# Pair-wise tap tables, wider tap matmuls and one-run Toeplitz loads in a kernel of attention and a state-space convolution

## The chip, the core and the metric

The kernel runs on one core of one Trainium2 chip. The metric is device time in microseconds for one launch, taken as the median of several runs. A profiled execution stands beside the runs; its span is what the views of the trace cover.

## What is computed

Sequence length 2,048, width 448. Two branches share the input layout and are mixed by a gate for each row (cut from the reference):

```python
g = sigmoid((x * gate_w).sum(-1, keepdims=True))
# branch A: attention, 16 query heads of 28 on one shared key and value head
scores = einsum("bhqd,bkd->bhqk", q, k) * 28 ** -0.5
a = (softmax(scores) @ v).reshape(B, S, 448) @ wo
# branch B: 448 channels, 256 complex modes each; taps K, then a causal convolution
P = exp((dt * (A_re + 1j * A_im))[:, :, None] * l)          # l = 0..2047
K = einsum("dn,dnl,dn->dl", Cc, P, dt * Bc).real
b = causal_conv(u, K) + u * Dskip                           # by FFT in the reference
out = g * a + (1 - g) * b
```

## The kernel before

All work is written as operations with dependences (`Prog.op`, `Prog.dma`), and `Prog.schedule` puts them into one fixed order per engine. It walks through the program with a planned duration for each operation and a priority `pr`; among what could start, the earliest goes first, and at equal times the lower `pr`. It also plans TensorE's code: instructions come in blocks of 256, and a new block is taken to need `FETCH` nanoseconds when the DMA is planned busy and `IDLE` when it is not (line 82, used in lines 201 to 221). Operations with `pr` of 1 or more may be held back for this. The engines then run their lists in order, with semaphore waits.

**Attention.** The scores of 16 row blocks (four heads of 512 rows each time) are cut into 1,024 tiles of 128 x 512. `qk` (lines 1095 to 1136) makes two or three tiles in up to five PSUM banks, on TensorE as 3 matmuls on 29 rows (line 1103) or as four column groups of 32 (line 1112); ScalarE takes the exponential of the two or three in one instruction (line 1134), and `pv` multiplies with the values (line 1144). VectorE evicts (line 1004) and scales by the denominators (line 1014), which take a detour through DRAM issued by GpSimd. `qproj` makes the queries (line 759), `outp` the output projection (line 986, folded in by line 995), three times four of them during the stream, and the fourth set in `tail` (line 1055).

**Taps.** The channels go in 14 blocks `c` of 32, with modes on the 128 partitions in two halves, so 64 columns for each power. `masters` (lines 780 to 818) squares the modes for a group of blocks. `tables(c)` builds, on VectorE, 32 powers by doubling: five levels `lv`, in each of which the existing `w` rows are multiplied by the real and imaginary master (lines 850 and 852) and combined (lines 854 and 856). `rho` (line 863) holds squared magnitudes, line 867 makes from it the second half of the moving operand, `Fm`, and line 872 turns the sign of the imaginary rows. In `tab` a row holds the 128 columns of one power, 256 bytes, so what one channel needs steps by 256 bytes.

`kgen(c)` (lines 875 to 912) turns the tables into taps: for each channel, over two halves of the modes and the real and imaginary part, a matmul with 32 stationary columns (one every row) and 64 moving ones. Four channels stand side by side in column groups of 32. That is 128 matmuls for 32 channels, all into one PSUM bank; VectorE adds the skip term (line 899) and evicts (line 902) into `kstg`, and nine transfers on GpSimd's queue write the taps to DRAM, in `KP_scratch`, which has a row of `KW` = 1,088 for each channel (and a shifted copy, `KH` further on).

**Convolution.** `tload` (lines 924 to 935) reads Toeplitz matrices from `KP_scratch`: four channels at a time, 128 partitions, each one element further into the row, as two transfers (even and odd partitions) of 64 partitions with four runs of 2,048 bytes. There are seven buffers (`tbufs`, lines 914 to 922): four in `T`, and three in `U` that come free as its channels are used up. 112 such loads are issued on SP's queue, in order, each when its buffer is free and its taps are in DRAM. `conv` (28 times, lines 937 to 978) runs 128 matmuls over four loads (line 949), scales (line 958), transposes back (line 969) and adds to `O` (line 977). It takes two of the two PSUM banks that groups share (`POOL`, line 85): one for the sums, one for the transposed result.

In the order of before the tap generation of the last block stands at exp tiles 940 to 955 of 1,024, and convolutions 22 and 23 of 0 to 27 at 925 to 940 and 960 to 968; convolutions 26 and 27 come after the last tile.

Of the kernel before, what the change touches and what calls it, by code (L numbers as in the profile page):

```python
# [24 lines left out]
BLK = 33 * EW  # L25
LO = 2 * BLK
# [8 lines left out]
TW = 4 * 1024  # L35
# [39 lines left out]
class Prog:  # L75
# [6 lines left out]
    BLOCK, FIRST, FETCH, IDLE, NEED = 256, 172, 5300.0, 3300.0, 0.015  # L82
# [48 lines left out]
    def dma(self, pairs, desc, slot, rd=(), wr=(), pr=0, eng="sp", slow=False, extra=0):  # L131
# [6 lines left out]
        o = self.op(eng, fn, nd * ns / 16.0 * (1.15 if size < 1500 else 1.8 if nd < 512 else 1.0), rd, wr, pr)  # L138
# [237 lines left out]
class Kernel:  # L376
# [25 lines left out]
    def alloc(self):  # L402
# [26 lines left out]
        self.T = sb("T", NTR * TW + 768, BF)  # L429
# [10 lines left out]
        self.kstg = sb("kstg", 2 * 256, BF)  # L440
# [44 lines left out]
    def loads(self):  # L485
# [62 lines left out]
        pg.dma([(self.skt.v(32 * g + 31, 1, 0, [[8, 14], [1, 8]]), dram(ins["B_Dskip"], 8 * g, [[16 * D, 1], [32, 14], [1, 8]]))  # L548
                for g in range(4)], (112, 8), "sk", rd=["skt"], wr=["skt"], pr=1, slow=True)
# [230 lines left out]
    def masters(self, b):  # L780
# [13 lines left out]
        for k in range(11):  # L794
# [20 lines left out]
            off = k * 256 if k < 5 else (k - 6) * 256 + 64  # L815
# [4 lines left out]
    def tables(self, c):  # L820
# [18 lines left out]
        done = [lk(1), lk(2)]
        for lv in range(5):  # L840
# [388 lines left out]
```

## Time and profile before

| | |
|---|---|
| median of 3 runs | 544.31 us (542.96 to 545.7) |
| profiled execution | 546.33 us; its span 544.5 us |
| granted TensorE clock, mean | 0.953 |
| ScalarE, exponentials (line 1134) | 410 instructions, 468.1 us |
| VectorE, busy | 455.3 us in 826 instructions |
| TensorE, tap generation (line 889) | 1,792 matmuls recorded |
| Toeplitz loads | 224 transfers of 512 KB, about 9.4 us from issue to landing |

The span is cut into 40 slices in the views that show digits; each digit is the busy share in tenths. A group's line gives the line in the code, engine, operation, what it writes and reads, shape, count, busy time, mean length in nanoseconds, and the idle time just before it with what ended it. "issue" is idle time for which the profile shows no one being waited for. Matmul lengths overlap each other; their pace is read from how long a row of them takes. "T<-KP_scratch" and "U<-KP_scratch" are the Toeplitz loads.

### The profile page before, as it was taken

The page shows a single profiled execution, that of the slowest core. Times are in us where ns is not written, and L with a number is a line of the kernel's source. Part 1 is how long each engine was busy: PE and PEld are TensorE (multiplying, and loading weights), DVE is VectorE, ACT ScalarE, POOL GpSimd, SP SyncE. Part 2 cuts the span into 40 slices and gives each one's busy share as a digit, 9 for nine tenths or more (in the row PEclk, how much of TensorE's full clock was granted, in tenths as well). Part 3 has the DMA queues.
Part 4 walks back from the last instruction along what each step waited for, and adds up shares of the span by engine and source line. Part 5 has one row for each costly group of instructions (what it writes and reads, how often), then busy time and mean ns, then how long its engine had stood idle before and what let it go on. Part 6 is the DMA issues. An engine that isn't in the chain of part 4 may idle for free.

```text
span 544.5 us, 20905 instructions
## 1 busy us (share of the span) xinstructions
PE 451.6 (83%) x9463; PEld 226.4 (42%) x9479; DVE 455.3 (84%) x826; ACT 485.9 (89%) x431; POOL 168.1 (31%) x313
## 2 busy tenths in 40 slices
PE   4787679688798989789788898889898898996875
PEld 3522114154353535345344445345454444352443
DVE  2889999999999989889989998989899999912024
ACT  3699899999999989899999999999999998997840
POOL 5017022515142413315215241515225060532100
PEclk9958888999999999899999999999899999998888
DMA  8995691696977697896994998798994999679996
GB/s 254 238 232 151 47 159 30 172 355 206 360 238 247 189 368 244 257 365 216 361 373 136 362 308 305 208 390 273 326 371 144 345 337 353 182 258 321 361 385 194
DMA packets 122401, 144.55 MB, mean 265 GB/s; under 512 B 54196, under 2 KB 60956, under 8 KB 122312
## 3 DMA queue, kind: packets, MB, share of 16 engines
q1 hardware_dynamic: 112312, 133.06, 75.9%
q0 software_dynamic: 9344, 9.59, 7.3%
q8 instruction: 74, 1.21, 0.9%
q10 hardware_dynamic: 656, 0.57, 0.4%
q14 instruction: 15, 0.12, 0.1%
HBM read 128.76 MB, written 5.28 MB: 246 GB/s over the span
## 4 chain that ended last, share of the span: by engine, by line
ACT 30%; PE 27%; DVE 19%; DMA 15%; issue 3%; SPq 0%
ACT expT L1134 30%; DMA T<-KP_scratch 9%; PE psS L1112 6%; DMA U<-KP_scratch 6%; PE psX L889 5%; PE psS L1103 4%; PE psB L1144 4%; PE psS L949 2%; PE psX L949 2%; DVE msq L796 2%; DVE tab L850 2%; DVE mbf L816 2%; DVE seedz L800 1%; PE psS L889 1%; DVE tmp L852 1%
## 5 line engine op out<-in xcount | busy, mean ns | idle before, releaser
L1134 ACT ACTIVATE expT<-psS 128x1536 bf16<-128x1536 f32 (+1 forms) x410 | 468.1, 1317 | 23.1 <-PE psS L1112 11.7
L1112 PE MATMUL psS<-qM,kT 128*32 128x512 bf16 x1660 | 134.3, 400 | 14.0 <-ACT expT L1134 10.6
L1103 PE MATMUL psS<-qT,kT 29*128 29x512 bf16 x609 | 82.9, 400 | 33.4 <-ACT expT L1134 29.6
L1144 PE MATMUL psB<-expT,vaug 128*32 128x512 bf16 x1024 | 104.7, 398 | 0.7 <-issue 0.4
L135 POOL DMA_DIRECT2D KP_scratch<-kstg x126 | 67.8, 546 | 70.7 <-DVE kstg L902 69.2
L850 DVE TENSOR_TENSOR tab<-tab,mbf 128x256 bf16<-128x256 bf16 (+4 forms) x70 | 68.6, 979 | 0.7
L1103 PEld LDWEIGHTS psS<-qT,kT 29*128 29x128 bf16 x609 | 19.9, 91 | 83.3 <-ACT expT L1134 72.9
L135 POOL DMA_DIRECT2D rdenB<-R_scratch x60 | 30.6, 517 | 75.8 <-DMA R_scratch<-denT 56.3
L889 PE MATMUL psX<-tab 128*32 128x64 bf16 x1280 | 49.5, 286 | 0.3 <-issue 0.2
L1112 PEld LDWEIGHTS psS<-qM,kT 128*32 128x32 bf16 x1660 | 30.4, 98 | 45.6 <-ACT expT L1134 34.7
L1144 PEld LDWEIGHTS psB<-expT,vaug 128*32 128x32 bf16 x1024 | 27.4, 96 | 49.9 <-issue 38.2
L135 POOL DMA_DIRECT2D qM<-qT x64 | 32.1, 509 | 43.4 <-DVE gt L638 20.4
L889 PEld LDWEIGHTS psX<-tab 128*32 128x32 bf16 x1280 | 39.4, 135 | 11.3 <-issue 3.9
L949 PE MATMUL psX<-T,U 128*32 128x128 bf16 (+7 forms) x1568 | 34.4, 221 | 9.0 <-DMA T<-KP_scratch 5.9
L135 POOL DMA_DIRECT2D denT<-acc x15 | 11.3, 756 | 97.5 <-DVE acc L1004 97.5
L949 PE MATMUL psS<-T,U 128*32 128x128 bf16 (+7 forms) x1216 | 30.2, 222 | 9.5 <-DMA T<-KP_scratch 6.7
L852 DVE TENSOR_TENSOR tmp<-tab,mbf 128x256 bf16<-128x256 bf16 (+3 forms) x56 | 36.3, 648 | 0.0
L949 PEld LDWEIGHTS psX<-T,U 128*32 128x32 bf16 (+7 forms) x1568 | 26.5, 94 | 20.3 <-DMA T<-KP_scratch 8.1
L867 DVE TENSOR_TENSOR tab<-tab,tmp 128x4096 bf16<-128x4096 bf16 x14 | 32.1, 2290 | 0.4
L852 DVE TENSOR_TENSOR tab<-tab,mbf 128x4096 bf16<-128x4096 bf16 x14 | 31.9, 2278 | 0.0
L949 PEld LDWEIGHTS psS<-T,U 128*32 128x32 bf16 (+7 forms) x1216 | 21.7, 95 | 21.0 <-DMA T<-KP_scratch 6.9
L863 DVE TENSOR_TENSOR tmp<-tmp,mq 128x64 bf16<-128x64 bf16 (+4 forms) x70 | 25.3, 361 | 1.2
(153 smaller groups left out, 553.4 us busy)
## 6 DMA issues: line engine op xcount, KB each, us to landing
T<-KP_scratch SPq DMA_DIRECT2D x174, 512.0 KB, 9.3
U<-KP_scratch SPq DMA_DIRECT2D x50, 512.0 KB, 9.5
rdenB<-R_scratch POOLq DMA_DIRECT2D x60, 64.0 KB
U<-cst SPq DMA_DIRECT2D x1, 3584.0 KB, 19.0
qM<-qT POOLq DMA_DIRECT2D x64, 32.0 KB, 5.2
tab<-in_A_x_dram SPq DMA_DIRECT2D x4, 448.0 KB, 6.2
O<-in_A_x_dram SPq DMA_DIRECT2D x16, 112.0 KB, 2.7
O<-cst SPq DMA_DIRECT2D x1, 1792.0 KB, 27.1
```

The costliest lines, as they stand in the source:

```text
L135: return [e.dma_start(o, i, **kw) for o, i in pairs]
L796: pg.op("dve", lambda e: e.tensor_tensor(m2(msq), z2, z2, ALU.mult), el(2 * n), rd=[kr, ki] + first, wr=["msq"], pr=pr)
L850: vo(lambda e, dst=dst, src=src, mr=mr: e.tensor_tensor(dst, src, mr, ALU.mult), 2 * n, done + mk(lv), [kr, ki])
L852: vo(lambda e, src=src, mi=mi, w=w, tb=tb, to=to: e.tensor_tensor(tb.v(0, P, to, [[w * EW, 2], [EW, w], [1, EW]]), src, mi, ALU.mult), 2 * ...
L863: vo(lambda e, w=w, lv=lv: e.tensor_tensor(rho.v(0, P, (32 - 2 * w) * 64, [[64, w], [1, 64]]), rho.v(0, P, (32 - w) * 64, [[64, w], [1, 64]]),
L867: vo(lambda e: e.tensor_tensor(tab.v(0, P, FM, [[64, 2], [EW, 32], [1, 64]]), tab.v(0, P, lo + 31 * EW, [[BLK, 2], [-EW, 32], [1, 64]]), r ...
L889: r = e.matmul(G.v(32 * g, 32, 64 * jj, [[1, 64]]), tab.v(0, P, lo + comp * BLK + 64 + o, [[EW, 32]]), tab.v(0, P, fo, [[mo - fo, 2], [EW, ...
L949: r = e.matmul(ps.v(32 * j, 32 - 2 * n, 128 * k, [[1, 128]]), self.U.v(0, P, (4 * gi + j) * 32 + 2 * n, [[1, 32 - 2 * n]]), tbuf.v(0, P, t ...
L1103: r = e.matmul(self.psS.v(0, P, 512 * b, [[1, 512]]), kT.v(32 * h, DH + 1, 128 * kt, [[1, 128]]), qT.v(32 * h, DH + 1, 512 * (i % 2), [[1, ...
L1112: r = e.matmul(self.psS.v(32 * j, 32, 512 * b, [[1, 512]]), kT.v(0, P, 128 * kt + 32 * j, [[1, 32]]), self.qM.v(0, P, (i % 2) * XQ + 512 * ...
L1134: pg.op("act", lambda e: e.activation(expT.v(0, P, 512 * es[0], spread(es, n)), self.psS.v(0, P, 512 * bs[0], spread(bs, n)), AF.Exp, scal ...
L1144: r = e.matmul(self.psB.v(32 * h, 32, 0, [[1, 512]]), vaug.v(0, P, 32 * kt, [[1, 32]]), expT.v(0, P, 512 * ring[t], [[1, 512]]), start=(kt ...
```

## The change

- **Layout of the tables.** Two channels' elements lie beside each other as a pair, then real and imaginary pairs, then the next power: what a channel needs steps by 4 elements (8 bytes), and a row of 128 holds 32 powers for one pair. All operands of `tables` get patterns that end in runs of two. The product into `Fm` is made in two instructions of 2,048 elements, and a small copy puts the first power in place.
- **Tap generation.** A matmul has 64 stationary and 128 moving columns, for two neighbouring pairs' channels at once on a column group of 64; the blocks off the diagonal of its result are not used. 64 matmuls for 32 channels, in two PSUM banks one after the other, each with its own skip addition and eviction; ten transfers instead of nine write the taps.
- **Toeplitz loads.** A load is one transfer; each of 128 partitions gets one run of 4,288 elements, 8,576 bytes, which takes the four rows together with the 64 elements between them.
- **Order.** `FETCH` goes from 5,300 to 6,200, output projections from priority 2 to 1.2, a convolution uses one PSUM bank, and the buffers in `U` come into use 8 loads later. The skip values are loaded as single elements in the new order of channels.

In the new order the last tap generation stands at exp tiles 956 to 971, convolution 23 at 936 to 961 and convolution 24 at 973 to 988. VectorE has 56 instructions more, TensorE 896 matmuls fewer (8,570), GpSimd's queue 14 transfers more, SP's queue 112 fewer.

```diff
-BLK = 33 * EW
-LO = 2 * BLK
+LO = 64 * EW + 8
...
-TW = 4 * 1024
+TW = 3 * KW + 1024
...
-    BLOCK, FIRST, FETCH, IDLE, NEED = 256, 172, 5300.0, 3300.0, 0.015
+    BLOCK, FIRST, FETCH, IDLE, NEED = 256, 172, 6200.0, 3300.0, 0.015
...
-        self.kstg = sb("kstg", 2 * 256, BF)
+        self.kstg = sb("kstg", 1024, BF)
...
-        pg.dma([(self.skt.v(32 * g + 31, 1, 0, [[8, 14], [1, 8]]), dram(ins["B_Dskip"], 8 * g, [[16 * D, 1], [32, 14], [1, 8]]))
-                for g in range(4)], (112, 8), "sk", rd=["skt"], wr=["skt"], pr=1, slow=True)
+        pg.dma([(self.skt.v(32 * g + 31, 1, 0, [[8, 14], [1, 8]]), dram(ins["B_Dskip"], 2 * (g % 2) + g // 2, [[16 * D, 1], [32, 14], [4, 8]]))
+                for g in range(4)], (448, 8), "sk", rd=["skt"], wr=["skt"], pr=1, slow=True)
...
-            o = s * LO + 32 * EW
+            o = s * LO + 64 * EW
-                pg.op("dve", lambda e, o=o, comp=comp, val=val: e.memset(self.tab.v(0, P, o + comp * BLK, [[1, 64]]), val), 70,
+                pg.op("dve", lambda e, o=o, comp=comp, val=val: e.memset(self.tab.v(0, P, o + 2 * comp, [[1, 2]]), val), 60,
...
-            off = k * 256 if k < 5 else (k - 6) * 256 + 64
+            off = k * 256 + 64 if k < 5 else (k - 6) * 256
...
-        mq = lambda lv: self.mq.v(0, P, lv * W2 + 64 * c, [[1, 64]])
+        mq = lambda lv: self.mq.v(0, P, lv * W2 + 64 * c, [[2, 32], [1, 2]])
-        vo(lambda e: e.tensor_copy(tab.v(0, P, lo + 31 * EW, [[BLK, 2], [1, 64]]), mbf.v(0, P, mo, [[128, 2], [1, 64]])),
+        lm = lo + 32 * EW
+        vo(lambda e: e.tensor_copy(tab.v(0, P, lm + 124, [[2, 2], [EW, 32], [1, 2]]), mbf.v(0, P, mo + 64, [[128, 2], [2, 32], [1, 2]])),
-        vo(lambda e: e.tensor_copy(tab.v(0, P, lo + 31 * EW + 64, [[BLK, 2], [1, 64]]),
-                                   self.seedw.v(0, P, c * 64, [[W2, 2], [1, 64]])),
+        vo(lambda e: e.tensor_copy(tab.v(0, P, lo + 124, [[2, 2], [EW, 32], [1, 2]]),
+                                   self.seedw.v(0, P, c * 64, [[W2, 2], [2, 32], [1, 2]])),
-            so, do = lo + (32 - w) * EW, lo + (32 - 2 * w) * EW
-            src = tab.v(0, P, so, [[BLK, 2], [EW, w], [1, EW]])
-            dst = tab.v(0, P, do, [[BLK, 2], [EW, w], [1, EW]])
-            mr = mbf.v(0, P, m, [[0, 2], [0, w], [1, EW]])
-            mi = mbf.v(0, P, m + 128, [[0, 2], [0, w], [1, EW]])
+            so, do = lo + (32 - w) * 4, lo + (32 - 2 * w) * 4
+            src = tab.v(0, P, so, [[EW, 64], [2, 2 * w], [1, 2]])
+            dst = tab.v(0, P, do, [[EW, 64], [2, 2 * w], [1, 2]])
+            dc = [tab.v(0, P, do + 2 * k, [[EW, 64], [4, w], [1, 2]]) for k in range(2)]
+            mr = mbf.v(0, P, m, [[2, 64], [0, 2 * w], [1, 2]])
+            mi = mbf.v(0, P, m + 128, [[2, 64], [0, 2 * w], [1, 2]])
-            vo(lambda e, src=src, mi=mi, w=w, tb=tb, to=to: e.tensor_tensor(
-                tb.v(0, P, to, [[w * EW, 2], [EW, w], [1, EW]]), src, mi, ALU.mult), 2 * n, done + mk(lv), [tk])
-            vo(lambda e, do=do, n=n, tb=tb, to=to: e.tensor_tensor(
-                tab.v(0, P, do, [[1, n]]), tab.v(0, P, do, [[1, n]]), tb.v(0, P, to + n, [[1, n]]), ALU.subtract), n, [tk, kr], [kr])
-            vo(lambda e, do=do, n=n, tb=tb, to=to: e.tensor_tensor(
-                tab.v(0, P, do + BLK, [[1, n]]), tab.v(0, P, do + BLK, [[1, n]]), tb.v(0, P, to, [[1, n]]), ALU.add), n, [tk, ki], [ki])
+            tv = tb.v(0, P, to, [[4 * w, 64], [2, 2 * w], [1, 2]])
+            tc = [tb.v(0, P, to + 2 * k, [[4 * w, 64], [4, w], [1, 2]]) for k in range(2)]
+            vo(lambda e, src=src, mi=mi, tv=tv: e.tensor_tensor(tv, src, mi, ALU.mult), 2 * n, done + mk(lv), [tk])
+            vo(lambda e, dc=dc, tc=tc: e.tensor_tensor(dc[0], dc[0], tc[1], ALU.subtract), n, [tk, kr], [kr])
+            vo(lambda e, dc=dc, tc=tc: e.tensor_tensor(dc[1], dc[1], tc[0], ALU.add), n, [tk, ki], [ki])
-        vo(lambda e: e.tensor_copy(rho.v(0, P, 31 * 64, [[1, 64]]), mq(0)), 64,
+        vo(lambda e: e.tensor_copy(rho.v(0, P, 62, [[64, 32], [1, 2]]), mq(0)), 64,
-            vo(lambda e, w=w, lv=lv: e.tensor_tensor(rho.v(0, P, (32 - 2 * w) * 64, [[64, w], [1, 64]]),
-                                                     rho.v(0, P, (32 - w) * 64, [[64, w], [1, 64]]),
-                                                     self.mq.v(0, P, lv * W2 + 64 * c, [[0, w], [1, 64]]), ALU.mult), w * 64,
+            vo(lambda e, w=w, lv=lv: e.tensor_tensor(rho.v(0, P, (32 - 2 * w) * 2, [[64, 32], [2, w], [1, 2]]),
+                                                     rho.v(0, P, (32 - w) * 2, [[64, 32], [2, w], [1, 2]]),
+                                                     self.mq.v(0, P, lv * W2 + 64 * c, [[2, 32], [0, w], [1, 2]]), ALU.mult), w * 64,
-        vo(lambda e: e.tensor_tensor(tab.v(0, P, FM, [[64, 2], [EW, 32], [1, 64]]),
-                                     tab.v(0, P, lo + 31 * EW, [[BLK, 2], [-EW, 32], [1, 64]]),
-                                     rho.v(0, P, 31 * 64, [[0, 2], [-64, 32], [1, 64]]), ALU.mult), 4096,
-           done + ["tmp"], ["Fm"])
-        ni = tab.v(0, P, lo + BLK + EW, [[EW, 31], [1, 64]])
+        for k in range(2):
+            vo(lambda e, k=k: e.tensor_tensor(tab.v(0, P, FM + 2 * k, [[EW, 32], [4, 32], [1, 2]]),
+                                              tab.v(0, P, lm + 124 + 2 * k, [[EW, 32], [-4, 32], [1, 2]]),
+                                              rho.v(0, P, 62, [[64, 32], [-2, 32], [1, 2]]), ALU.mult), 2048,
+               done + ["tmp"], ["Fm"])
+        vo(lambda e: e.tensor_copy(tab.v(0, P, lm + EW, [[EW, 31], [1, 4]]), tab.v(0, P, lo + 64 * EW, [[0, 31], [1, 4]])),
+           124, done + ["Fm"], done)
+        ni = tab.v(0, P, lm + 6, [[EW, 32], [4, 31], [1, 2]])
...
-        for jj in range(8):
...
-                            G.v(32 * g, 32, 64 * jj, [[1, 64]]),
-                            tab.v(0, P, lo + comp * BLK + 64 + o, [[EW, 32]]),
-                            tab.v(0, P, fo, [[mo - fo, 2], [EW, 32]]),
...
+        for q in range(2):
+            G = self.grp()
+            for k in range(4):
+                m = 4 * q + k
+
+                def mm(e, m=m, k=k, G=G):
+                    for comp in range(2):
+                        for half in range(2):
+                            for u in range(2):
+                                cg = half * 16 + 2 * m
+                                fo = lo + (32 + cg) * EW + 4 + 2 * comp + u
+                                mo = FM + cg * EW + 2 * comp + u
+                                r = e.matmul(
+                                    G.v(64 * u, 64, 128 * k, [[1, 128]]),
+                                    tab.v(0, P, lo + cg * EW + 2 * comp + u, [[4, 64]]),
+                                    tab.v(0, P, fo, [[EW, 2], [mo - fo, 2], [4, 32]]),
+                                    start=(comp == 0 and half == 0), stop=(comp == 1 and half == 1),
+                                    tile_position=(0, 64 * u), skip_group_check=True)
+                    return r
+                pg.op("pe", mm, 230, mode="h", ni=16, rd=keys,
+                      wr=[(X, q), ("kst", q), ("ksk", q)], pr=1.4, lock=G if k == 0 else None)
+            o = 512 * q
+            pg.op("dve", lambda e, o=o, q=q, G=G: e.tensor_tensor(
+                ko.v(0, P, o + 63, [[128, 4], [64, 2]]), G.v(0, P, 63, [[128, 4], [64, 2]]),
+                self.skt.v(0, P, 8 * c + 4 * q, [[1, 4], [0, 2]]), ALU.add),
+                el(8), rd=[(X, q), "skt"], wr=[("ksk", q)], pr=2)
+            pg.op("dve", lambda e, o=o, G=G: e.tensor_copy(ko.v(0, P, o, [[64, 8], [1, 63]]), G.v(0, P, 0, [[64, 8], [1, 63]])),
+                  el(504), rd=[(X, q)], wr=[("kst", q)], pr=2, unlock=G)
+        lst = [(dram(self.KP, (32 * c + 2 * b) * KW + 1024, [[KW, 2], [4 * KW, 8], [1, 64]]),
+                bass.AP(tensor=ko.h, offset=(16 + 32 * b) * rs + 64 * b, ap=[[64 * rs, 2], [128, 8], [1, 64]])) for b in range(2)]
-                lst.append((dram(self.KP, h * KH + (32 * c + 8 * g) * KW, [[64, 16], [KW, 8], [1, 64]]),
-                            ko.v(32 * g + 16 * h, 16, 0, [[64, 8], [1, 64]])))
-        pg.dma(lst, (1056, 128), "kw", rd=["kst", "kst2"], wr=[("KP", c)], pr=0, eng="pool", extra=4000)
+                lst.append((dram(self.KP, h * KH + (32 * c + 2 * (g % 2) + g // 2) * KW, [[64, 16], [4 * KW, 8], [1, 64]]),
+                            ko.v(32 * g + 16 * h, 16, 64 * (g % 2), [[128, 8], [1, 64]])))
+        pg.dma(lst, (1056, 128), "kw", rd=[("kst", q) for q in range(2)] + [("ksk", q) for q in range(2)],
+               wr=[("KP", c)], pr=0, eng="pool", extra=4000)
-        home = [(self.T, k * TW, 0) for k in range(NTR)] + [(self.U, k * TW, (k + 1) * 32) for k in range(3)]
+        home = [(self.T, k * TW, 0) for k in range(NTR)] + [(self.U, k * TW, 8 + (k + 1) * 32) for k in range(3)]
...
-        lst = []
-        for h in range(2):
-            to = bass.AP(tensor=buf.h, offset=h * buf.rs + o, ap=[[2 * buf.rs, 64], [1024, 4], [1, 1024]])
-            lst.append((to, dram(self.KP, h * KH + 4 * gi * KW, [[1, 64], [KW, 4], [1, 1024]])))
-        self.lastT = pg.dma(lst, (512, 2048), f"T{s}", rd=[("KP", gi // 8), "pad"] + x, wr=w, pr=1, extra=1500).i
+        self.lastT = pg.dma([(buf.v(0, P, o, [[1, TW]]), dram(self.KP, 4 * gi * KW, [[1, 64], [KH, 2], [1, TW]]))], (128, 2 * TW), f"T{s}", rd=[("KP", gi // 8), "pad"] + x, wr=w, pr=1, extra=1500).i
-        ps, px = self.grp(), self.grp()
+        ps = px = self.grp()
...
-                                     tbuf.v(0, P, to + j * 1024 + 896 - 128 * n, [[1, 128]]),
+                                     tbuf.v(0, P, to + j * KW + 896 - 128 * n, [[1, 128]]),
...
-              el(512), rd=[X, "omq"], wr=[("cst", cs)], pr=2, unlock=ps)
+              el(512), rd=[X, "omq"], wr=[("cst", cs), X], pr=2)
...
-            pg.op("pe", lambda e, k=k: yt(e, k), 70, mode="h", ni=8, rd=[("cst", cs), "id"], wr=[Y], pr=1.55, lock=px if k == 0 else None)
+            pg.op("pe", lambda e, k=k: yt(e, k), 70, mode="h", ni=8, rd=[("cst", cs), "id"], wr=[Y], pr=1.55)
...
-                rd=["Wo"] + [("on", gg) for gg in range(4)], wr=[X], pr=2, lock=G if g == 0 else None)
+                rd=["Wo"] + [("on", gg) for gg in range(4)], wr=[X], pr=1.2, lock=G if g == 0 else None)
```

More of the change, by code (lines that the diff above doesn't have):

```diff
@@ L137, in dma @@
         ns = 10.0 if size < 64 else 13.0 + 0.033 * size if size < 1500 else 8.0 + 0.0372 * size
-        o = self.op(eng, fn, nd * ns / 16.0 * (1.15 if size < 1500 else 1.8 if nd < 512 else 1.0), rd, wr, pr)
+        o = self.op(eng, fn, nd * ns / 16.0 * (1.15 if size < 1500 else 1.8 if size < 8000 and nd < 512 else 1.0), rd, wr, pr)
         o.slot, o.ndma, o.extra = slot, len(pairs), extra
@@ L428, in alloc @@
         self.O = sb("O", 16 * D, BF)
-        self.T = sb("T", NTR * TW + 768, BF)
+        self.T = sb("T", NTR * TW, BF)
         self.tab = sb("tab", 2 * LO + 32 * EW, BF)
@@ L642, in xq @@
     def xq(self, q):
-        return ((self.xT, 0), (self.T, NTR * TW + 768 - XQ), (self.expT, 9 * 512), (self.expT, 5 * 512))[q]
+        return ((self.xT, 0), (self.T, NTR * TW - XQ), (self.expT, 9 * 512), (self.expT, 5 * 512))[q]
     def xk(self, q):
@@ L879, in kgen @@
         X = ("kx", c)
-        G = self.grp()
         keys = self.tabkeys
-        for jj in range(8):
-            def mm(e, comp, jj=jj):
-                for half in range(2):
-                    for g in range(4):
-                        o = half * 32 + 8 * g + jj
-                        fo = lo + comp * BLK + EW + o
-                        mo = FM + comp * 64 + o
-                        r = e.matmul(
-                            G.v(32 * g, 32, 64 * jj, [[1, 64]]),
-                            tab.v(0, P, lo + comp * BLK + 64 + o, [[EW, 32]]),
-                            tab.v(0, P, fo, [[mo - fo, 2], [EW, 32]]),
-                            start=(comp == 0 and half == 0), stop=(comp == 1 and half == 1),
-                            tile_position=(0, 32 * g), skip_group_check=True)
-                return r
-            for comp in range(2):
-                pg.op("pe", lambda e, mm=mm, comp=comp: mm(e, comp), 226, mode="c", ni=16, rd=keys,
-                      wr=[X, "kst", "kst2"], pr=1.4, lock=G if jj == 0 and comp == 0 else None)
@@ L899, in kgen @@
-        pg.op("dve", lambda e: e.tensor_tensor(self.kstg.v(0, P, 63, [[64, 8]]), G.v(0, P, 63, [[64, 8]]),
-                                               self.skt.v(0, P, 8 * c, [[1, 8]]), ALU.add),
-              el(8), rd=[X, "skt"], wr=["kst"], pr=2)
-        pg.op("dve", lambda e: e.tensor_copy(self.kstg.v(0, P, 0, [[64, 8], [1, 63]]), G.v(0, P, 0, [[64, 8], [1, 63]])),
-              el(504), rd=[X], wr=["kst2"], pr=2, unlock=G)
         ko = self.kstg
         rs = ko.rs
-        lst = [(dram(self.KP, 32 * c * KW + 1024, [[8 * KW, 4], [KW, 8], [1, 64]]),
-                bass.AP(tensor=ko.h, offset=16 * rs, ap=[[32 * rs, 4], [64, 8], [1, 64]]))]
+        for q in range(2):
[25 more added lines that the diff above has]
+                  el(504), rd=[(X, q)], wr=[("kst", q)], pr=2, unlock=G)
```

## The prediction, made before the changed kernel ran

> **What bounds the kernel now.** I read the busy shares and the slices first, then the queues, then the groups, then the last third in the windows and the timeline.
>
> ```profile
> PE 451.6 (83%) x9463; PEld 226.4 (42%) x9479; DVE 455.3 (84%) x826; ACT 485.9 (89%) x431; POOL 168.1 (31%) x313
> ...
> DVE  2889999999999989889989998989899999912024
> ACT  3699899999999989899999999999999998997840
> ...
> DMA  8995691696977697896994998798994999679996
> ...
> q1 hardware_dynamic: 112312, 133.06, 75.9%
> ...
> q8 instruction: 74, 1.21, 0.9%
> ```
>
> VectorE and ScalarE are both at 9 from slice 4 on; VectorE falls off at slice 35 (476 us), ScalarE at slice 38. ScalarE's exp groups are 468.1 us for 1,024 tiles, 0.457 us a tile, and the change does not touch them. So the time is when the exp stream starts, its idle time, and what lies behind it. Queue q8 brings TensorE's code: 18,942 instructions over 74 packets is 256 a packet. In the trace's packet records 68 of the 74 lie after 100 us, 6.4 us apart on average and never under 3.5. TensorE's idle time called "issue" is where this bites:
>
> ```profile
> 454.01 0.61 PE L1112 MATMUL psS<-qM,kT 128*32 128x512 bf16 x7
> 455.72 0.38 PE L1112 MATMUL psS<-qM,kT 128*32 128x512 bf16 x1 [1.10 <-issue]
> ...
> 459.65 0.62 PE L889 MATMUL psX<-tab 128*32 128x64 bf16 x16
> ...
> 460.74 0.23 PE L949 MATMUL psS<-T,U 128*32 128x128 bf16 x1
> 462.04 0.40 PE L949 MATMUL psS<-T,U 128*32 128x128 bf16 x15 [1.06 <-issue]
> ```
>
> The two stops are 256 instructions apart, and each ends 1.3 to 1.6 us after a q8 packet has landed. I find some fifteen such stops; about 7 us of ScalarE's idle time before 476 us and about half of VectorE's fall on them. The last third by stage:
>
> ```profile
> 340.00:476.00 136.00, 120.73 (x2754) 61.24 (x2755) 127.84 (x222) 130.63 (x116) 49.01 (x91) 0.99 0.88 292
> 476.00:523.00 47.00, 38.30 (x898) 19.35 (x895) 8.82 (x17) 41.40 (x37) 10.04 (x19) 0.93 0.95 321
> ```
>
> Columns: TensorE, its weight loads, VectorE, ScalarE, GpSimd, granted clock, DMA share, GB/s. Up to 476 us VectorE has 8.2 us of slack in 136 and the DMA 12%; then VectorE is done, the DMA share is 0.95, and ScalarE idles 5.6 us of 47. So VectorE's table work sets when the last taps exist, and then the last Toeplitz loads and the exp stream race to the end.
>
> **The change part by part.**
>
> ```profile
> L889 PE MATMUL psX<-tab 128*32 128x64 bf16 x1280 | 49.5, 286 | 0.3 <-issue 0.2
> ...
> L867 DVE TENSOR_TENSOR tab<-tab,tmp 128x4096 bf16<-128x4096 bf16 x14 | 32.1, 2290 | 0.4
> L850 DVE TENSOR_TENSOR tab<-tab,mbf 128x4096 bf16<-128x4096 bf16 x14 | 32.0, 2288 | 0.1
> ```
>
> *VectorE, more instructions.* Per channel block (14 of them) a second pair of evictions, 186 + 673 ns (L899, L902); the product of L867 in two halves, 2 x 1,212 (L854 with 2,048) - 2,290 = 134 ns; one small copy, 186 ns (L836). Together 1.18 us, 16.5 us in all, 56 instructions. It lies on the path, since VectorE is full.
>
> *VectorE, new patterns.* The tables now lie as pairs: every operand runs over two elements and then steps. No row of before shows runs of two. The nearest, L867, reads runs of 64 backwards and takes what L850 takes over straight rows, so steps between runs cost nothing there: lower end 0. Upper end: the pair rate is lost, as for PSUM sources (L958, 512 elements, 683 ns against 423 for L863): 0.51 ns an element over 29,900 elements a block, 15 us a block, 213 us. I take 0, since each run is still one whole pair as in L867, and keep the far end as a case.
>
> *TensorE, tap generation.* Now 128 matmuls a block at 28 ns (24 in 0.84 us, 8 in 0.39), 3.6 us. Afterwards 64 with 128 moving columns on two column groups. L889 spends 1.75 ns a column and group, with a step of 256 bytes; L949, contiguous, 0.43 (13.9 ns per matmul on four groups); L969, step 4 bytes on two groups, 0.5. The new step is 8 bytes. Ends: 64 x 128 x 0.43 / 2 = 1.76 us and 64 x 128 x 1.75 / 2 = 7.2 us. I take L969's rate, 2.05 us: 1.5 us less a block, 22 us of a TensorE that is 83% busy; the high end would add 50 us. The Trainium skill (SBUF — State Buffer, section "Door 1: The DMA port swizzle") says that two hits in a 16-byte line suffice for full rate, which would make it 1.76 us; no run yet shows an 8-byte step.
>
> *Code.* 896 matmuls fewer are 1,792 instructions, 7 of the 74 blocks: 61 instead of 68 after 100 us. At 6.4 us that is 45 us of refilling that TensorE no longer waits for or spaces itself around. The order also allows 6.2 us instead of 5.3 for a refill beside DMA traffic, nearer to the 6.1 us or so between block crossings where it stalled.
>
> *Toeplitz loads.* By the packet records 2,048 bytes take 85 ns, 4,096 take 159: 0.0366 ns a byte and 10 ns more. A run of 8,576 then takes 324 ns. A load is 32 x 85 = 2.72 us per engine before and 8 x 324 = 2.59 after, with 4.7% more bytes: 0.13 us less, 14.5 us over 112 loads. Other end: the 2,048-byte rate stays (0.0415), 2.85 us, 14.5 us more. SP issues 112 transfers instead of 224; it waits for slots anyway, so 0.
>
> *A rule against it.* The two parts meet at q8: a refill shares the engines with the loads. Today half a load puts 16 x 85 = 1.36 us on an engine; the new one puts 8 x 324 = 2.59. The Trainium skill (DMA: Bandwidth & Descriptors, section "Queues, rings and completion order") says that an engine changes between queues only at packet ends, so longer runs would delay each refill; no run here shows it.
>
> *Small edits.* GpSimd issues ten transfers of taps instead of nine: 0.55 us, once on the path of the last block. The skip values come as 448 single elements; the first tap generation is at 84 us, hidden. A convolution uses one PSUM bank instead of two; the other bank hides its wait, and if not, 28 times the 0.4 us of L977. Output projections move up: the third set stands at tiles 840 to 865 instead of 868 to 970, out of the last stretch.
>
> *The order.* The last tap generation stands at exp tiles 956 to 971 instead of 940 to 955, but convolution 24 then follows at once. With seven buffers, 9 loads instead of 13 are left behind it.
>
> *Sum.* The last table ended at 476.4; plus 16.5, less 8 us of VectorE waits that the code stops caused: 484.9. Tap generation starts 0.8 later, 485.7, at tile 956. The other 68 tiles are 31.1 us; idle time between was 7.6 us (46.0 us for 84 tiles), with four loads fewer I take 2: exp ends at 518.8. What followed was 21.3 us; less 2 for convolutions that wait for no load: 538.1. The loads check: taps done at 493, in DRAM at 503, 9 loads of 2.6 to 526.5, then 9 us as before, 535.5: not later. Against the span of 544.5 that is 6.4 us less; the profiled execution took 546.33, so 539.9, and the median of the runs lies 0.4% under the profiled one: 538 us.
>
> **The rivals.**
>
> *Refills slow down (slower).* Place: TensorE's block ends. 61 blocks fit into the 438 us after 100 us at 7.2 us each; beyond that TensorE's code sets the time. With 6.1 plus the 1.23 us of longer queueing it is 7.3 and 550 to 552; a second such wait gives 8.5 and over 600. For it: stops exist already. Against it: 7 blocks fewer and a more careful order. Chance 0.22.
>
> *VectorE alone decides (no change).* Its waits stay, the 16.5 us come in full: the last table at 493, span 546, median 545. For it: VectorE's slack is 21 us from 100 to 476, and part of that is waits for attention. 0.13.
>
> *The pairs cost.* Whole rate lost: over 740, 0.04. A few per cent of the 20.7 us a block, some 9 us: 549, 0.04.
>
> *More is freed.* If exp loses nearly all its idle time, it ends near 512 and the whole at 529 to 532. For it: TensorE loses 22 us of work as well as its stops. 0.20.
>
> **How the numbers follow.** My forecast has 0.37; its own range is 533 to 541.5. About 0.5% is what a measurement of this kernel can tell from no change. Faster by more: 0.37 + 0.20 = 0.57; within it: 0.13; slower: 0.22 + 0.04 + 0.04 = 0.30. From 524 to 557, what is left out is the worse half of the refill case, the lost pair rate and a little below: under 0.2.
>
> **What would show it.** Right: about 67 packets on q8, 6 to 7 us apart, few "issue" stops; the tap line at about 30 ns a matmul; table groups unchanged within 2%; T packets of 8,576 bytes near 324 ns; VectorE's drop at about 485 us. Wrong: q8 packets over 7.2 us apart with TensorE idle before them, table groups of 4,096 well over 2.29 us, or a tap matmul of over 55 ns.

## The result, and the profile after

The changed kernel takes 569.25 us (median of 4, 566.86 to 571.63) against 544.65 us for the one before in the same runs: a ratio of 1.0455, with a 95% interval of 1.0403 to 1.0506. It is slower by 24.6 us; the profiled execution took 569.09 us with a span of 567.2.

The page of the changed kernel, with the lines that answer to those of before:

```profile
PE 469.9 (83%) x8567; PEld 224.0 (39%) x8583; DVE 469.4 (83%) x882; ACT 489.3 (86%) x431; POOL 175.3 (31%) x327
...
DVE  4989999989999999799888989899999989851131
ACT  4789899989989999799888999999999993999900
...
q8 instruction: 67, 1.10, 0.8%
```

There are 896 matmuls fewer, and yet TensorE is busy 18 us longer. VectorE has 14.1 us more. ScalarE dips to 7 and 8 in the middle of the span and to 3 in slice 34, and stops two slices before the end. (The granted clock, 0.925 to 0.940 in the four runs, is no explanation of that size: the runs of the kernel before that stand beside the experiments took 540.7 to 549.6 us at 0.924 to 0.956.) The windows, cut at the last table and the last exponential:

```profile
340.00:502.60 162.60, 141.72 (x2951) 69.88 (x2953) 151.35 (x280) 147.97 (x130) 55.58 (x105) 0.98 0.86 318
502.60:538.50 35.90, 28.46 (x630) 14.63 (x630) 6.39 (x13) 33.67 (x31) 8.57 (x16) 0.97 0.91 342
538.50:567.20 28.70, 15.44 (x324) 10.39 (x324) 7.03 (x12) 0.01 (x1) 0.00 (x0) 0.68 0.68 230
```

The last table is done at 502.6 (476.4 before), the exp stream ends at 538.5 (523.2), and what follows takes 28.7 us (21.3). From 340 us to the last table VectorE has 11 us of slack in 163, about the share of before, but ScalarE has 15, where it had 5 in 136. What the exponentials waited for, in the view of the waits, first before, then after:

```profile
ACT expT L1134 <- PE psS L1112: 11.7, 13, 2.4
ACT expT L1134 <- PE psS L1103: 8.3, 12, 1.5
```

```profile
ACT expT L1139 <- PE psS L1108: 20.4, 33, 1.6
ACT expT L1139 <- PE psS L1117: 16.1, 20, 4.8
```

Total, times and longest in us: scores came late for 36.5 us instead of 20.0. VectorE waits too: ahead of its first instruction on a finished bank of taps (L908, L899 in the kernel before) it stood idle behind tap matmuls for 23.9 us, 7.2 before, and of the 26.2 us by which the last table is later, 16.6 are VectorE's added busy time and 9.6 its added idle time. So TensorE holds both back, and here is with what (page, groups; busy time and mean ns, then the idle time before):

```profile
L898 PE MATMUL psS<-tab 128*64 128x128 bf16 x544 | 40.5, 302 | 0.0
L898 PE MATMUL psX<-tab 128*64 128x128 bf16 x352 | 27.1, 303 | 0.7 <-DVE tab L875 0.7
```

Together 67.6 us where before it was 69.0 (49.5 + 19.5) for twice as many. (These lengths overlap other matmuls. Without the tap groups TensorE is busy for 411 and 412 us; the taps add 40 before and 58 after.) The mean from start to start inside a chunk is 57.7 ns for a tap matmul, before it was 23, so a block needs 64 x 57.7 = 3.7 us instead of 128 x 23 = 2.9. This measure leaves out the last pair, or group of four, of each chunk; from pair to pair it is 62 ns, and before from four to four 27, near the prediction's 28; by these a block needs 4.0 us instead of 3.5. The prediction had 2.05 us for after. The paces below are start to start.

### The profile page after: what moved, and what is told of

Its sections match the earlier page's. It is cut to its first block, busy times and chain, and to the rows that moved or that the text cites. A ratio compares the mean times of both kernels' runs of the same rounds, so it can differ in the third digit from the quotient of the medians.

```text
span 567.2 us, 19071 instructions
## 1 busy us (share of the span) xinstructions
PE 469.9 (83%) x8567; PEld 224.0 (39%) x8583; DVE 469.4 (83%) x882; ACT 489.3 (86%) x431; POOL 175.3 (31%) x327
## 4 chain that ended last, share of the span: by engine, by line
ACT 42%; PE 32%; DMA 11%; DVE 7%; POOL 1%; issue 1%
ACT expT L1139 42%; DMA T<-KP_scratch 8%; PE psS L898 6%; PE psS L1117 6%; PE psS L1108 4%; PE psX L898 4%; PE psB L1149 4%; PE psX L954 2%; DMA rdenB<-R_scratch 2%; PE psS L954 2%; DMA U<-KP_scratch 1%; POOL KP_scratch L134 1%; PE psX L991 1%; DVE msq L795 1%; DVE seedz L797 1%; DVE seedz L799 1%
## 5 line engine op out<-in xcount | busy, mean ns | idle before, releaser
L1139 ACT ACTIVATE expT<-psS 128x1024 bf16<-128x1024 f32 (+1 forms) x410 | 471.5, 1286 | 38.1 <-PE psS L1108 20.4
L1117 PE MATMUL psS<-qM,kT 128*32 128x512 bf16 x1660 | 136.9, 410 | 19.8 <-ACT expT L1139 18.5
L134 POOL DMA_DIRECT2D KP_scratch<-kstg x140 | 75.4, 546 | 72.6 <-DVE kstg L912 70.2
L1117 PEld LDWEIGHTS psS<-qM,kT 128*32 128x32 bf16 x1660 | 28.5, 98 | 61.0 <-ACT expT L1139 49.0
L954 PE MATMUL psX<-T,U 128*32 128x128 bf16 (+7 forms) x1600 | 40.2, 228 | 2.9 <-DMA T<-KP_scratch 2.3
L898 PE MATMUL psS<-tab 128*64 128x128 bf16 x544 | 40.5, 302 | 0.0
L954 PEld LDWEIGHTS psX<-T,U 128*32 128x32 bf16 (+7 forms) x1600 | 29.9, 98 | 20.5 <-issue 8.4
L855 DVE TENSOR_TENSOR tmp<-tab,mbf 128x256 bf16<-128x256 bf16 (+3 forms) x56 | 36.5, 653 | 0.0
L898 PEld LDWEIGHTS psS<-tab 128*64 128x64 bf16 x544 | 30.0, 140 | 12.8 <-issue 8.7
L868 DVE TENSOR_TENSOR tab<-tab,tmp 128x2048 bf16<-128x2048 bf16 x28 | 34.3, 1224 | 0.7
L954 PE MATMUL psS<-T,U 128*18 128x128 bf16 (+7 forms) x1280 | 29.1, 222 | 6.6 <-DMA T<-KP_scratch 5.5
L134 POOL DMA_DIRECT2D R_scratch<-denT x15 | 8.6, 576 | 81.6 <-DVE denT L1015 34.4
L898 PE MATMUL psX<-tab 128*64 128x128 bf16 x352 | 27.1, 303 | 0.7 <-DVE tab L875 0.7
## 6 DMA issues: line engine op xcount, KB each, us to landing
U<-cst SPq DMA_DIRECT2D x1, 3584.0 KB, 19.5
```

The source lines that it names most:

```text
L134: return [e.dma_start(o, i, **kw) for o, i in pairs]
L855: vo(lambda e, src=src, mi=mi, tv=tv: e.tensor_tensor(tv, src, mi, ALU.mult), 2 * n, done + mk(lv), [tk])
L868: vo(lambda e, k=k: e.tensor_tensor(tab.v(0, P, FM + 2 * k, [[EW, 32], [4, 32], [1, 2]]), tab.v(0, P, lm + 124 + 2 * k, [[EW, 32], [-4, 32 ...
L898: r = e.matmul(G.v(64 * u, 64, 128 * k, [[1, 128]]), tab.v(0, P, lo + cg * EW + 2 * comp + u, [[4, 64]]), tab.v(0, P, fo, [[EW, 2], [mo - ...
L954: r = e.matmul(ps.v(32 * j, 32 - 2 * n, 128 * k, [[1, 128]]), self.U.v(0, P, (4 * gi + j) * 32 + 2 * n, [[1, 32 - 2 * n]]), tbuf.v(0, P, t ...
L1117: r = e.matmul(self.psS.v(32 * j, 32, 512 * b, [[1, 512]]), kT.v(0, P, 128 * kt + 32 * j, [[1, 32]]), self.qM.v(0, P, (i % 2) * XQ + 512 * ...
```

## The experiments

The theory after the result (A): the tap matmul at a step of 8 bytes is slow, and the order, which counts on 29 ns for it, packs it between score groups. Rivals: long runs in the loads (C), VectorE's added work alone (D), and the order at the end. Each kernel is compared with the one before on its own chip, medians 544.6 to 545.4 (546.45 for e13's single run).

**e1, four forms of operands.** In the changed kernel:

```diff
-  tab.v(0, P, lo + cg * EW + 2 * comp + u, [[4, 64]]),
+  tab.v(0, P, lo + cg * EW + (64 * comp if c % 4 in (2, 3) else 2 * comp + u), [[1 if c % 4 in (2, 3) else 4, 64]]),
-  tab.v(0, P, fo, [[EW, 2], [mo - fo, 2], [4, 32]]),
+  tab.v(0, P, fo, [[EW, 2], [mo - fo, 2], [1 if c % 4 in (1, 3) else 4, 32]]),
```

> The changed kernel, with the operands of the tap matmuls in four forms by channel block c % 4: 0 as changed (both step 8 bytes), 1 moving columns contiguous, 2 stationary columns contiguous, 3 both contiguous; the taps of forms 1 to 3 are not the right ones. Theory A (the 8-byte step of an operand sets the pace): the pace inside a chunk is 58 ns a matmul in form 0 and about 28 ns in form 3, and forms 1 and 2 say which operand it is. Rival B (two column groups of 64 do not run beside each other, so 128 columns at 0.43 ns come one after the other): 55 to 58 ns in all four. Time: 560 to 569 us by A, 569 by B.

Measured, start to start: 58 to 60 ns as changed, 33 with contiguous moving columns, 54 to 56 with contiguous stationary ones, 30 with both. One run, 557.5 us, below the 560 that A gave. So it is the moving operand's step; the two column groups do run beside each other (B falls), and the stationary operand's step costs 2 to 3 ns.

**e2, both contiguous everywhere.**

```diff
-  tab.v(0, P, lo + cg * EW + 2 * comp + u, [[4, 64]]),
-  tab.v(0, P, fo, [[EW, 2], [mo - fo, 2], [4, 32]]),
+  tab.v(0, P, lo + cg * EW + 64 * comp, [[1, 64]]),
+  tab.v(0, P, fo, [[EW, 2], [mo - fo, 2], [1, 32]]),
```

> The changed kernel with both operands of every tap matmul contiguous (wrong taps, same count, same order of instructions). Theory A (the slow tap matmuls, planned at 29 ns and taking 58, hold the exp stream back): 28 ns a matmul, TensorE freed of 1.9 us a block, 26 us in all; ScalarE's wait for scores falls from 36.5 us toward the 20 of before; 550 to 556 us. Rival C (the long runs of the loads): no more than 3 us less, 566 to 570. Rival D (VectorE's added 16.5 us): 562 to 567.

Measured: 551.33 us (547.85 to 553.42), ratio 1.0108 [1.0074, 1.0142]. 17.9 us of the 24.6 are the pace of these matmuls. ScalarE's waits for scores fall from 36.5 to 23.2 us, the last table comes at 485.9, the last exponential ends at 521.3. VectorE's added work, given as D, cannot do that: it is the same here. What falls is VectorE's wait for tap matmuls, from 23.9 to 9.1 us. But the tail stays at 28 us.

**e3, the planner told.**

```diff
-  pg.op("pe", mm, 230, mode="h", ni=16, rd=keys,
+  pg.op("pe", mm, 461, mode="h", ni=16, rd=keys,
```

> The changed kernel with the planned duration of a chunk of 8 tap matmuls at 461 ns instead of 230; the order is planned anew, the work is the same. If packing too many tap matmuls between two score groups is what stops ScalarE, its wait for scores falls by some 8 to 10 us and the time is 556 to 562. If it is the work itself or VectorE, 565 to 571. The pace of the tap matmul stays at 58 ns.

Measured: 562.87 us (559.85 to 566.9). The waits for scores fall further than expected, to 10.3 us (6.3 + 4.0), and the exp stream ends at 512.7, 10.5 us earlier than before the change. The time hardly follows, 0.9 us above the interval that I gave: the new order spreads the last taps over more exp tiles, the last eviction of taps starts at 501.4, and the tail is 45 us. Exp time that is bought by delaying taps is given back at the end.

**e4, the loads of before in the changed kernel.** `tload` as before, and with it (the size of `T` and one place in it follow and are left out here):

```diff
-TW = 3 * KW + 1024
+TW = 4 * 1024
-  [(self.U, k * TW, 8 + (k + 1) * 32) for k in range(3)]
+  [(self.U, k * TW, (k + 1) * 32) for k in range(3)]
-  tbuf.v(0, P, to + j * KW + 896 - 128 * n, [[1, 128]])
+  tbuf.v(0, P, to + j * 1024 + 896 - 128 * n, [[1, 128]])
```

> The changed kernel with the loads of before: two transfers of 64 partitions with four runs of 2,048 bytes, and the buffer places of before. Rival C (a load of long runs delays code refills, or the last load comes late by its buffers): 548 to 556, q8 packets closer together. Theory A and D: 566 to 572; the last load, which is issued at 552 us in the changed kernel, may move by a few us with the new order.

Measured: 565.7 us (562.8 to 567.84), 3.5 us under the changed kernel and just below what A and D gave; nowhere near C. The order differs too, so this alone does not settle it.

**e5, VectorE's work alone, in the kernel before.**

```diff
-  vo(lambda e: e.tensor_tensor(tab.v(0, P, FM, [[64, 2], [EW, 32], [1, 64]]),
+  for k in range(2):
+      vo(lambda e, k=k: e.tensor_tensor(tab.v(0, P, FM + 64 * k, [[EW, 32], [1, 64]]),
...
+  vo(lambda e: e.tensor_copy(tab.v(0, P, lo + 31 * EW, [[4, 31], [1, 4]]), tab.v(0, P, lo + 31 * EW, [[4, 31], [1, 4]])), 124,
...
+  pg.op("dve", lambda e: e.tensor_tensor(self.kstg.v(0, P, 63, [[64, 8]]), G.v(0, P, 63, [[64, 8]]),
+  pg.op("dve", lambda e: e.tensor_copy(self.kstg.v(0, P, 0, [[64, 8], [1, 63]]), G.v(0, P, 0, [[64, 8], [1, 63]])),
```

> The kernel before with VectorE's added work alone, 4 instructions a block: both evictions a second time, the product into Fm in two halves and a copy of 124 elements onto itself; 1.18 us a block, 16.5 in all. Theory A+D (the added VectorE work is on the path, but part of it goes into its idle time, as e2 shows with the last table at 485.9 instead of 476.4): the last table at 484 to 488, 551 to 556 us. If VectorE's idle time took it in: 545 to 548. If all of it counted: 560 to 562.

Measured: 560.75 us (558.66 to 562.53), ratio 1.0296 [1.025, 1.0342]: 16.2 us by the medians, the case in which all of the 16.5 count. The expectation that idle time takes a part was wrong: the last table comes at 497.1, far later than the 484 to 488 expected and 20.7 us later than before, 15.4 of it busy time. But the exp stream ends at 522.9, as before; all of the added time lies behind it (35.4 us instead of 21.3). The order was planned anew too, so that 16.2 comes so near to 16.5 may be chance.

**e6, the new loads alone, in the kernel before.** The edit of e4 the other way round, and the planner's price for the transfer:

```diff
...
-  1.8 if nd < 512 else 1.0
+  1.8 if size < 8000 and nd < 512 else 1.0
...
```

> The kernel before with the loads of the change alone: one transfer with 128 runs of 8,576 bytes, the buffer places 8 loads later and the planner's price for it. If the long runs cost nothing by themselves: 542 to 548, the T packets at 324 to 330 ns, q8 packets as far apart as before. Rival C (code refills behind the long runs): 550 to 556. The prediction's 14.5 us less of DMA time would give 540 to 543.

Measured: 565.25 us (561.07 to 569.2), far above all three. The exp stream is 3.3 us later than before up to tile 704 and 23.2 us at tile 736: one stop. TensorE's timeline, and ScalarE's line after it:

```profile
384.63 1.67 PE L982 MATMUL psX<-Wo,onT 128*128 128x448 bf16 x4 [1.42 <-DVE O L973]
387.92 1.05 PE L945 MATMUL psS<-T,U 128*32 128x128 bf16 x32 [1.61 <-DMA T<-KP_scratch]
391.24 1.05 PE L945 MATMUL psS<-U 128*32 128x128 bf16 x32 [2.27 <-DMA U<-KP_scratch]
394.09 1.05 PE L945 MATMUL psS<-T,U 128*32 128x128 bf16 x32 [1.81 <-DMA T<-KP_scratch]
```

```profile
395.61 3.28 ACT L1130 ACTIVATE expT<-psS 128x1024 bf16<-128x1024 f32 x3 [19.26 <-PE psB L1140]
```

The new order puts an output projection and three loads' worth of convolution ahead of the next attention work, and TensorE, which takes its list in order, waits for each load in turn. So the stop comes from what this order puts there; e6 alone does not show whether shorter runs would have come sooner, which e10 and e12 take up. TensorE's "issue" stops are 12.5 us in 17 pieces, 12.1 in 17 before, and the q8 packets 6.5 us apart instead of 6.4: C finds no support.

**e7, another PSUM bank for the fourth output projection.**

```diff
...
-  G = self.grp()
-  px = lambda: G.v(0, P, 0, [[1, D]])
...
+  t, o = self.bank((2 + tt) % 5)
+  px = lambda t=t, o=o: t.v(0, P, o, [[1, D]])
...
```

> The changed kernel with the fourth of the last output projections in one of the score banks instead of one of the two shared PSUM banks. If the end is late because convolution 26 waits for that bank, and with it the buffer of load 112, then that load is issued some 8 us earlier than 552 and the time is 560 to 564. If the loads alone set the end: 567 to 571, as the changed kernel.

Measured: 565.86 us (564.07 to 569.01), between the two ranges, and the last load still issued at 551.2. The bank is not what the end waits for; this idea fell.

**e8, the refill's price.**

```diff
-  256, 172, 6200.0, 3300.0, 0.015
+  256, 172, 5300.0, 3300.0, 0.015
```

> The changed kernel with the planner's price for a code refill at 5,300 ns as before. If the order's more careful spacing costs exp time: 562 to 566. If it saves: 572 to 576. By theory A it decides little: 566 to 572, with the tap matmul at 58 ns.

Measured: 564.12 us (563.84 to 565.9), 5.1 us less. In the order with 6,200, exp tiles 896 to 928 contain a stop; the changed kernel's timeline there:

```profile
474.25 0.63 PE L954 MATMUL psS<-T,U 128*32 128x128 bf16 x32 [1.22 <-DMA T<-KP_scratch]
...
477.37 1.02 ACT L1139 ACTIVATE expT<-psS 128x1024 bf16<-128x1024 f32 x1 [4.79 <-PE psS L1117]
...
478.06 2.16 PE L898 MATMUL psX<-tab 128*64 128x128 bf16 x32 [0.74 <-DVE tab L875]
...
481.24 2.37 ACT L1139 ACTIVATE expT<-psS 128x1024 bf16<-128x1024 f32 x2 [2.85 <-PE psS L1117]
```

A convolution waits for its load in front of the scores, and then 32 tap matmuls stand in one piece: 2.16 us where the planner counted 0.92. ScalarE loses 4.8, 2.9 and, just after, 0.8 us. With 5,300 the stop is gone: its waits for L1117 are 6.1 us instead of 16.1. The time falls into the first range, but by luck: expected was an effect of the refills' spacing; what came was another place for one stop. Part of the stop may be the clock: from 475.2 to 482.1 us the granted clock was 0.51, eight score matmuls took 1.04 us instead of 0.61, and e8 has no such stretch there. The two are not separated.

**e9, the third buffer in `U` from load 110 on.**

```diff
-  [(self.U, k * TW, 8 + (k + 1) * 32) for k in range(3)]
+  [(self.U, k * TW, (40, 72, 110)[k]) for k in range(3)]
```

> The changed kernel with the third buffer in U coming into use at load 110 instead of 104, so that load 104, the first of convolution 26, goes into a buffer that is free earlier; the last loads are then not chained over convolution 25, load 104, convolution 26 and load 111. Theory T (that chain makes the tail 28.7 us instead of 21.3): the last load is issued before 540 us instead of 552, time 560 to 564. Rival (the tail is VectorE's and the output projections): 567 to 571.

Measured: 561.83 us (561.28 to 564.2), 7.4 us less. SP's queue at the end of the changed kernel, then of e9:

```profile
530.15 2.27 SPq L134 DMA_DIRECT2D U<-KP_scratch  x2
532.46 1.00 SPq L134 DMA_DIRECT2D T<-KP_scratch  x1
552.17 0.51 SPq L134 DMA_DIRECT2D U<-KP_scratch  x1
```

```profile
532.99 1.21 SPq L134 DMA_DIRECT2D U<-KP_scratch  x1
534.24 0.60 SPq L134 DMA_DIRECT2D T<-KP_scratch  x1
```

A run of 8,576 bytes is wider than four of 2,048, so the buffers in `U` come into use 8 loads later, the third exactly at load 104, the first of convolution 26. It lies on columns that convolution 25 still needs, so load 104 is sent after loads 105 to 109, convolution 26 starts at 551.5 behind the output projections, and load 111, which goes into the same buffer, leaves at 552.2. In e9 the last load leaves at 534.2, 18 us earlier; it queues behind the others and lands at 552.7 instead of 559.9, nearly all of the 7.4 us, and the tail is 20.6 us.

**e10, the edits of e8 and e9; e11, those of e2, e8 and e9; e12, those of e4 and e8.**

> The changed kernel with that buffer place and with a refill priced at 5,300 ns as before. e8 showed the price alone at 564, without the stop of the exp stream at tile 905. If the two effects are separate: 556 to 560. If the tail's gain is the same time as the stop's: 562 to 565. The tap matmul stays at 58 ns and VectorE's last table at 503 to 505.

> As e10_home_fetch, and the tap matmuls with contiguous operands (wrong taps). With the three causes found taken away, the prediction's sum should hold: last table at 484 to 487, end of the exp stream at 515 to 519, 538 to 543 us. If something else is missing in the sum: 546 to 551.

> The changed kernel with the loads and buffers of before and a refill priced at 5,300 ns: the order has no planned stop, as e10_home_fetch has none, so the two differ by the loads. If long runs cost nothing: within 3 us of e10_home_fetch. Rival C (long runs delay code refills): 5 to 12 us below it. The prediction's term (long runs save 14.5 us of DMA time, partly on the path): 3 to 8 us above it.

Measured: e10 561.43 us (559.47 to 563.02), e11 545.26 us (543.0 to 548.56; ratio to before 1.0005 [0.9975, 1.0035]), e12 561.95 us (560.87 to 564.22). Three things follow. The stop and the late buffer are not additive: either gives 5 to 7 us, both together 8. Long runs cost nothing and bring nothing: e10 and e12 differ by 0.5 us, 1.0284 [1.0236, 1.0332] and 1.0301 [1.0253, 1.0349], though the packets of queue q1 take 70.7% of the engines' span in e10 and 73.9% in e12, some 18 us less. And with everything else equal the pace of the tap matmul is 16.2 us (e10 to e11). VectorE carries it: it waits for the taps, first in e10, then in e11,

```profile
DVE kstg L908 <- PE psS L898: 12.7, 11, 4.1
DVE kstg L908 <- PE psX L898: 12.0, 12, 3.0
```

```profile
DVE kstg L908 <- PE psS L898: 3.3, 4, 1.7
DVE kstg L908 <- PE psX L898: 2.4, 2, 2.0
```

24.7 us instead of 5.7, and the last table comes at 504.9 instead of 488.9: the same 16 us as in the time. e11 lies between its two ranges: the exp stream ends at 515.1 as expected, the last table came at 488.9, not 487, and from the start of the last eviction of taps to the end it took 48.0 us.

**e13, the step.**

```diff
-  tab.v(0, P, fo, [[EW, 2], [mo - fo, 2], [4, 32]]),
+  tab.v(0, P, fo, [[EW, 2], [mo - fo, 2], [c % 5, 32]]) if c % 5 else tab.v(0, P, fo - u, [[EW, 2], [4, 32], [1, 2]]),
```

> The changed kernel with the moving operand of the tap matmuls in five forms by channel block c % 5: steps of 1, 2, 3 and 4 elements (2, 4, 6 and 8 bytes), and for 0 runs of two elements every 8 bytes; only the step of 4 gives the right taps. e1 gave 30 to 33 ns contiguous and 56 to 58 at a step of 8 bytes. If the pace goes with the bytes passed over: about 33, 38, 47 and 57 ns, and 38 for the pairs. If only the 8-byte step falls out: 31 to 33 for steps 1 to 3, 57 for step 4, and 31 to 33 for the pairs. The time says nothing new, 553 to 562.

One run, 558.4 us. TensorE's timeline, 16 matmuls each, in order of time: the form in pairs, then steps of 1, 2, 4 and 3 elements:

```profile
84.71 0.70 PE L898 MATMUL psX<-tab 128*64 128x128 bf16 x16
...
115.11 0.71 PE L898 MATMUL psS<-tab 128*64 128x128 bf16 x16
...
153.52 0.73 PE L898 MATMUL psS<-tab 128*64 128x128 bf16 x16
...
207.80 1.18 PE L898 MATMUL psS<-tab 128*64 128x128 bf16 x16
...
349.81 0.97 PE L898 MATMUL psX<-tab 128*64 128x128 bf16 x16
```

Start to start at steps of 1, 2, 3 and 4 it is 33 to 34, 34 to 35, 47 and 57 to 59 ns; 33 for the pairs. (Three of the fourteen blocks are left out, the first with pairs, the first with a step of 3 and the last with a step of 2, with means of 41, 49 and 43: they lie in part where the granted clock was 0.51, 0.50 and 0.51, at 79.5 to 83.0, 171.7 to 178.5 and 465.2 to 472.1 us.) So 4 bytes are still nearly free, 6 are not, and pairs every 8 bytes are; neither expectation holds whole.

**e14, the step removed with the right taps.** 128 matmuls of 32 stationary columns on four groups; the moving operand takes both channels of a pair:

```diff
-  tab.v(0, P, lo + cg * EW + 2 * comp + u, [[4, 64]]),
-  tab.v(0, P, fo, [[EW, 2], [mo - fo, 2], [4, 32]]),
+  tab.v(0, P, lo + row * EW + 2 * comp + u, [[4, 32]]),
+  tab.v(0, P, fo, [[mo - fo, 2], [4, 32], [1, 2]]),
```

> The changed kernel (buffer place and refill price as in e10_home_fetch) with 128 tap matmuls a block of 32 stationary columns on four column groups; the moving operand takes both channels of a pair, in runs of two elements every 8 bytes, the eviction sorts the two channels apart. All taps are right. e13 gave 33 ns a matmul for such runs on two groups; on four the convolutions' 13.9 ns should come, 1.8 us a block instead of 3.7. If the pace is what counts and code is not: 545 to 550, close to e11. If the 896 matmuls of code that come back cost: 552 to 558. If the eviction, which now reads the sums with a step of 8 bytes, is slower than 673 ns: later by 28 times that.

Measured: 565.46 us (564.15 to 567.2), 15 us above the first range and 7 above the second. The pace came (14 to 17 ns, 1.9 us a block), and the eviction takes 674 to 676 ns. Still it is slower than e10. TensorE's stops called "issue", before, in the changed kernel and here (longest groups):

```profile
PE psS L949 <- issue: 4.2, 5, 1.1
PE psX L949 <- issue: 2.8, 6, 1.3
```

```profile
PE psX L954 <- issue: 0.5, 2, 0.3
```

```profile
PE psX L955 <- issue: 6.5, 3, 2.5
PE psS L1118 <- issue: 6.4, 4, 2.6
```

In all 12.1 us, 1.3 us and 24.2 us, with 74, 67 and 74 packets on q8. e11 has 67 packets, 9.0 us, and nearly the same matmul time a block, and is 20 us faster. The orders differ too, so how much of the 20 us is code is not shown.

None of these kernels beats the one before; e11, which does not compute the right taps, equals it. The earlier output projections and the single PSUM bank of a convolution were not tried alone.

## Why the prediction was wrong

Predicted 538.0 us, 524 to 557; measured 569.25. Three differences lead from one to the other: e11 stands 7.3 us above the forecast, the pace of the tap matmul adds 16.2 (e11 to e10), and the order and the buffers add 7.8 (e10 to the changed kernel). By the prediction's own steps:

- **VectorE, more instructions: the size right, the path only in part.** 16.5 us predicted; up to the last table VectorE's busy time is 16.6 us more as changed, 16.2 in e11. e5 is 16.2 us slower, but behind the exp stream, not through it. The 8 us taken off for waits that would go were too many: with the tap pace repaired (e11) the last table comes 12.5 us later than before, so 4 us went; as changed it comes 26.2 us later.
- **VectorE, new patterns: right.** The products of 4,096 take 2,288 ns as before, the halves 1,224 against 1,212. Only operations on 64 to 128 elements grew clearly, a copy for instance from 186 to 239 ns.
- **TensorE, tap generation: the step that failed.** Predicted 2.05 us a block from L969's rate at a step of 4 bytes, 1.5 us less than before; measured 3.7 to 4.0, and no less than before. For a step of 4 bytes the rate was right (34 to 35 ns in e13 make 2.2 us a block); it does not carry over to 8. The far end, 7.2, was in the text, but it was kept neither as a rival nor in the range. The sign named at the end, "a tap matmul of over 55 ns", is what came. The matmul's real pace against the one that e11 has is worth 16 to 18 us of the time (e10 to e11, changed kernel to e2), most of it through VectorE's wait for taps, while the sum had VectorE's waits falling. The rule weighed there, from the Trainium skill (SBUF — State Buffer, "Door 1: The DMA port swizzle"), that two hits in a line of 16 bytes give the full rate, does not hold for this operand: two hits (8 bytes) take 57 to 59 ns, four (4 bytes) 34 to 35. That sentence of the text was no part of its sum.
- **Code: the count right, its worth open.** 67 packets, and 1.3 us of stops instead of 12.1. But e11, with the same 67 and the faster matmuls, has 9.0 us of stops, so fewer blocks alone do not take them away. The packets are 7.5 us apart; the text named more than 7.2 with TensorE idle as the refill rival's sign, and TensorE is not idle: it runs more slowly through fewer instructions. e11 has VectorE's added work and is 15.5 us below e5, but tap pace, count, loads and order all differ, so the part of the fewer matmuls is not shown.
- **Loads: right.** Packets of 8,576 bytes take 326 ns (324 predicted), and nothing follows on the path (e10, e12). The rival that long runs hold up refills, with the rule on packet ends behind it, found no support: 12.5 us of stops in e6.
- **Small edits and the order: wrong.** The buffers' later use was told and not costed: 7.4 us by e9. The stop at tiles 896 to 928 was not foreseen; 5.1 us by e8, 8 with the first. The sum had idle time falling by 5.6 us and the tail by 2; the tail grew by 7.4.
- **The load check** had 42.5 us from the last taps to the end. In e9, e10 and e11 it is 46.8, 47.6 and 48.0 from the start of the last eviction (0.7 less from its end): the writes of taps take 12 to 13 us until the first load leaves, not 10; the last load lands 27 to 28 us after that, where nine at 2.6 us make 23.4, though only eight are left; and the end comes 7 us later, not 9. The check called this chain no later than the exp stream. In e11 it decides: the exp stream ends at 515.1, earlier than the 518.8 of the sum, and the span is 542.1, not 538.1.

None of the rivals had this: the pairs' cost was sought on VectorE, and the range ended at the half of the refill case.

With the tap pace repaired and the order mended, the measured value is 545, the figure of the rival "VectorE alone decides", but not by its way: 4 us of VectorE's waits did go, and the last loads took the time back. The gain that was predicted would not have come even then.

## What to carry to other kernels

Price a strided TensorE operand from a row with the same step, and where there is none keep the far end as a case with a chance of its own. In an order written out from planned durations a wrong price does harm twice, as time and as place: compare the planned duration with the trace. For the end of such a kernel, follow the last block: in e9 to e11 the span was the start of the last eviction of taps plus 47 to 48 us, while the exp stream ended 21 to 27 us before it.

## What the runs showed of the hardware

TensorE's moving operand in 2-byte elements: a matmul of 128 columns on two groups took 33 to 34 ns when contiguous, 34 to 35 at a step of 4 bytes, 47 at 6, 57 to 59 at 8, and 33 for pairs of elements every 8 bytes; a step of 8 bytes in the stationary operand cost 2 to 3 ns. The pace at a step of 8 bytes did not follow the granted clock: 32 matmuls took 2.17 us at 1.0 (e13, at 204.16 us) and 2.16 at 0.51 (changed kernel, 478.06). The contiguous form did: 24 took 0.96 us at 1.0 (e13, 118.52) and 32 took 1.92 at 0.50 (e2, 461.82). DMA packets of 8,576 bytes took 326 ns in the median, 0.038 ns a byte, against 0.0415 for 2,048, and this bought no time.
